# First batch's queries ahead of its keys and values, in an attention and gated feed-forward kernel on one core

## The chip, the cores and the metric

The kernel runs on one core of one Trainium2 chip. The core has five engines with instruction queues of their own: TensorE (PE in the profile, its weight loads PEld), VectorE (DVE), ScalarE (ACT), GpSimd (POOL) and SyncE (SP), which here only issues transfers. Sixteen DMA engines move data between HBM and the core's memory. The metric is device time in microseconds, the median of several runs.

## The reference, cut to what matters

```python
batch, n_heads, seq, head_dim = (8, 8, 576, 64)      # q, k, v, float32

kv  = np.einsum('bhsd,bhse->bhde', k, v)             # one 64x64 state per batch and head
out = np.einsum('bhsd,bhde->bhse', q, kv)
rms = np.sqrt(np.mean(out * out, axis=-1, keepdims=True) + 1e-06)
attn = out / rms * g_norm

x   = attn.transpose(0, 2, 1, 3).reshape(4608, 512)
rms = np.sqrt(np.mean(x * x, axis=-1, keepdims=True) + 1e-06)
xn  = x / rms * rms_g
g   = xn @ w_gate                                    # 512 x 1536
silu = g * (1.0 / (1.0 + np.exp(-g)))
y   = (silu * (xn @ w_val)) @ w_out                  # 1536 x 512
```

There is no softmax: keys and values of a head collapse into a 64x64 state, and each query row is multiplied by it. Two root-mean-square norms follow, one over a head and one over a token, and then a gated feed-forward layer.

## The kernel before, in words

The work goes through nine blocks of 512 tokens: the first 512 tokens of each of the eight batches, and a ninth block of the eight batches' last 64 tokens. For a block n the class `Ffn` computes twelve strips of gate and value products (`up`, L490, matmuls on L496), the gated product (L501 on ScalarE, L502 on VectorE), and four row blocks of down products (`down_products`, L543, matmuls on L548). While one block is in its feed-forward stage, the attention of the next is woven into it. Matrix products take bfloat16 operands, so every loaded float32 tile is cast once, on an engine that each call names.

The order of instructions on each engine is the order of the calls in the program (`tc.manual_schedule()`); nothing is reordered. Semaphores are put in by the framework: a reader waits for the writer of its tile, a tile that takes a pool buffer waits for the last user of that buffer, and a transfer on the hardware queues of SP or ACT waits for the eighth such transfer before it. Which buffer of a pool a tile gets is settled at build time.

The change lies in the start, before the first block's feed-forward stage. There the first batch is handled in pieces:

- Keys and values come in four pairs of heads, j = 0 to 3, 288 KB each (`load_kv`, L118). The first two pairs' keys go on SP's queue and their values on ScalarE's; the later two pairs go on SP's queue alone. `cast_kv` (L122) casts one pair.
- `state0(j, dummies)` (L681) takes a bank of `att_pool`, which has two, puts filler matmuls into it (`warm`, L646, on zeros), and multiplies the pair's keys and values in 18 matmuls of 64x64 (`kv_pair`, L251, matmuls on L256). With dummies = 0 it puts one narrow filler. `put_state0` (L687) copies the state out on VectorE.
- The first 256 queries of the batch come in two transfers of 256 KB (`load_q0(0, ...)`, L609), are cast on VectorE and ScalarE (`cast_q0`), turned by eight matmuls into an `att_pool` bank behind some fillers (`turn_q0`, L665), and put in place by one copy on VectorE and one on ScalarE (`put_q0`, L675). The second 256 queries go the same way later (`load_q0(1, ...)`).
- `columns(A, j, bank)` (L690) multiplies state j by the turned queries; `squares` and `square` square them on ScalarE; `A.sums()` adds the squares up with matmuls; `A.factors()` (L451) makes the norm factors; `scale_both` and `x_turn` then make the first feed-forward input. `Z` is the same for the second 256 queries.
- `gam` holds the two norm weights, turned by one small matmul (L742); from it come `gcol`, `rowscale` (L744) and `gsq`. `rowscale` multiplies every gate and value weight when it is rounded to bfloat16 (`round_w`, L186, on GpSimd L193, ScalarE L191 or VectorE L193).
- The weights follow on SP's queue in pieces of 512 KB and 1 MB (`load_w`, L169): first the strips 0 to 3 of gate (L180) and value (L184), then strips 4 to 7, then the rest, and after them the keys, values and queries of the next batches and the down weights (`load_wo`, L197).

Loaded float32 tiles live in a pool of seven `stage` buffers. The keys and values of the third batch are loaded by `load_pair(2)`, into buffers that earlier loads have left; VectorE and GpSimd cast them at 54 to 60 us.

Of the kernel before, what the change touches and what calls it, by code (L numbers as in the profile page):

```python
# [20 lines left out]
def kernel(  # L21
# [12 lines left out]
    nc = tc.nc  # L34
# [41 lines left out]
    PE, DVE, SC, GP = nc.tensor, nc.vector, nc.scalar, nc.gpsimd  # L76
# [26 lines left out]
    def cast(engine, dst, src):  # L103
        if engine is SC:
            engine.copy(out=dst, in_=src)  # L105
        else:
            engine.tensor_copy(out=dst, in_=src)  # L107
# [10 lines left out]
    def load_kv(b, name, queue, js=slice(0, NS)):  # L118
        view = srcs[name][b].rearrange("h s d -> (h s d)").rearrange("(j p x) -> p j x", j=NS, p=128)
        queue.dma_start(out=raws[b, name][:, js, :], in_=view[:, js, :])  # L120

    def cast_kv(b, name, j, engine, lo=0, hi=C):  # L122

        cast(
            engine, bufs[b][name][:, j, lo:hi].rearrange("p c d -> p (c d)"), raws[b, name][:, j, lo * D : hi * D]
        )
# [124 lines left out]
    def kv_pair(ps, j):  # L251

        for c in range(C):
            for u in range(2):
                rows = slice(u * D, u * D + D)
                PE.matmul(  # L256
                    ps[rows, rows], lhsT=kbs[0][rows, j, c, :], rhs=vbs[0][rows, j, c, :],
                    start=(c == 0), stop=(c == C - 1),
                )
# [349 lines left out]
    def load_q0(f, queue):  # L609

        src = q[0, :, 256 * f : 256 * f + 256, :].rearrange("(g h) (p t) d -> h p g (t d)", h=2, t=8)
        for h in range(2):
            queue.dma_start(out=q0[:, f, h, :], in_=src[h])

    for j in (0, 1):
        load_kv(0, "k", nc.sync, slice(j, j + 1))
        load_kv(0, "v", nc.scalar, slice(j, j + 1))
# [3 lines left out]
        out=gam[NS : NS + 1, :].rearrange("o (i d) -> o i d", i=2),  # L621
        in_=g_norm.rearrange("(o d) -> o d", o=1).unsqueeze(1).to_broadcast([1, 2, D]),
    )
    load_q0(0, nc.sync)
    for j in (2, 3):
        load_kv(0, "k", nc.sync, slice(j, j + 1))
        load_kv(0, "v", nc.sync, slice(j, j + 1))
# [18 lines left out]
    def warm(ps, count, w=512):  # L646
        for _ in range(count):
            PE.matmul(ps[:, 0:w], lhsT=warm_sb[:, 0:128], rhs=warm_sb[:, 0:w], start=True, stop=True, skip_group_check=True)  # L648
# [8 lines left out]
    A = Cols(0, 0, 256, qt0, sqt0, "A")  # L657
# [4 lines left out]
    def cast_q0(f, hs, engine):  # L662
        cast(engine, qb0[:, f, :, hs, :], q0[:, f, hs, :].rearrange("p h (t d) -> p t h d", t=8))

    def turn_q0(f, dummies):  # L665
        bank = att_pool.tile([128, 512], FP32, name="att_ps")
        warm(bank, dummies)
        ps = bank.bitcast(BF16).rearrange("p (t x) -> p t x", t=8)
        for t in range(8):
            PE.matmul(  # L670
                ps[:, t, :], lhsT=qb0[:, f, t], rhs=identity, is_transpose=True, start=(t == 0), stop=(t == 7),
            )
        return ps.rearrange("p t (x g) -> p g t x", g=NS)

    def put_q0(f, ps, i, engine):  # L675

        js = slice(2 * i, 2 * i + 2)
        dst = qt0[:, js, 256 * f : 256 * f + 256].rearrange("p j (t x) -> p j t x", t=8)
        cast(engine, dst, ps[:, js])

    def state0(j, dummies):  # L681
        ps = att_pool.tile([128, 512], FP32, name="att_ps")
        warm(ps, max(dummies, 1), 512 if dummies else 128)
        kv_pair(ps[:, 0:128], j)
        return ps

    def put_state0(j, ps):  # L687
        DVE.tensor_copy(out=kv_all[:, 0, j, :], in_=ps[:, 0:128])

    def columns(cols, j, bank):  # L690
        cols.turned(j, bank[:, 256 * (j % 2) : 256 * (j % 2) + 256])
# [6 lines left out]
    def squares(cols, i, bank):  # L698
        SC.activation(
            out=cols.sq[:, 2 * i : 2 * i + 2, :], in_=bank.rearrange("p (j t) -> p j t", j=2), func=ACT.Square  # L700
        )
# [16 lines left out]
    warm_ps = att_pool.tile([128, 512], FP32, name="att_ps")  # L718
    warm(warm_ps, 9)

    for j in (0, 1):
        cast_kv(0, "k", j, DVE)
        cast_kv(0, "v", j, SC)
    kv0 = state0(0, 0)
    kv1 = state0(1, 3)
    put_state0(0, kv0)
    cast_q0(0, hs0, DVE)
    cast_q0(0, hs1, SC)
    put_state0(1, kv1)
    banksA = [gps_pool.tile([128, MAIN], FP32, name="g_ps"), vps_pool.tile([128, MAIN], FP32, name="v_ps")]  # L730
    qps = turn_q0(0, 2)
    cast_kv(0, "k", 2, DVE)
    cast_kv(0, "v", 2, SC)
    put_q0(0, qps, 0, DVE)
    put_q0(0, qps, 1, SC)
    kv2 = state0(2, 3)
    cast_kv(0, "k", 3, DVE)
    put_state0(2, kv2)
    cast_kv(0, "v", 3, DVE, 0, 5)
    cast_kv(0, "v", 3, SC, 5, C)  # L740
    gam_ps = ops_pool.tile([128, 512], FP32, name="o_ps")
    PE.matmul(gam_ps[:, 0:5], lhsT=gam[0:5, :], rhs=ident32[0:5, 0:5], is_transpose=True, start=True, stop=True)  # L742
    DVE.tensor_copy(out=gcol, in_=gam_ps[:, NS : NS + 1])
    DVE.tensor_scalar(out=rowscale, in0=gam_ps[:, 0:NS], scalar1=gcol[:, 0:1], scalar2=None, op0=OP.mult)  # L744
    columns(A, 0, banksA[0])
    columns(A, 1, banksA[0])
    squares(A, 0, banksA[0])
    columns(A, 2, banksA[1])
    square(A, 2, banksA[1])
    kv3 = state0(3, 1)  # L750
# [17 lines left out]
    qps = turn_q0(1, 2)  # L768
# [336 lines left out]
```

## Time and profile before

| what | value |
|---|---|
| median of 5 runs | 319.05 us (318.86 to 319.52) |
| profiled execution, its own time | 319.15 us |
| its span, first to last instruction | 317.0 us |
| TensorE matmuls busy | 307.8 us, 97% of the span |
| VectorE, ScalarE, GpSimd busy | 179.8, 175.9, 22.7 us |
| moved by DMA | 54.95 MB, mean 173 GB/s |
| mean granted TensorE clock | 0.998 |

The span runs from the first to the last instruction; some 2 us of the run lie around it. A busy TensorE is pipelined work with modelled ends, so 97% says that the engine is hardly ever without work, not that it runs at its peak. In the lists of instructions each row gives a start, a length, the engine, the line of the program, the operation with its output and inputs, and in brackets the idle time of that engine just before it with what ended it. An engine name with a q (SPq) is the engine's queue issuing a transfer; a row named DMA in the chain is the time in which a transfer was under way.

### The profile page before, as it was taken

Reading aid. Unit: us, or ns where it says so; the run is one execution under the profiler, and the core shown is the slowest. Engines: PE = TensorE matmul, PEld = TensorE weight load, DVE = VectorE, ACT = ScalarE, POOL = GpSimd, SP = SyncE. Lnnn points to the kernel's source line nnn. Section 1 sums busy time; section 2 is a strip of 40 time slices with the busy share of each in tenths; the row PEclk is TensorE's granted clock in tenths of the full one; section 3 lists DMA queues with packets and bytes.
Section 4 is the critical chain, followed back from the end, with each engine's and each line's share of the span. In section 5 each row is a group of like instructions: output and inputs, shape, how many; then the busy total and the mean of one; then the engine's idle time right before and its main releaser. Section 6 shows DMA issues by size and latency. Waiting matters only on the chain.

```text
span 317.0 us, 6005 instructions
## 1 busy us (share of the span) xinstructions
PE 307.8 (97%) x2339; PEld 150.5 (47%) x2371; DVE 179.8 (57%) x373; ACT 175.9 (55%) x330; POOL 22.7 (7%) x48
## 2 busy tenths in 40 slices
PE   7899999999999999999999999999999999999995
PEld 3575446444454444444454445444444444444443
DVE  3666768679628922893179416950795079504310
ACT  3677367485878466837683768442744274233321
POOL 2264351100000000000000000000000000000000
PEclk9999999999999999999999999999999999999999
DMA  7999998699669347904790469136003710330014
GB/s 266 379 387 388 375 374 321 162 338 341 158 178 329 128 93 223 373 15 83 205 380 31 71 196 216 52 66 183 18 0 66 153 48 3 63 137 3 0 33 99
DMA packets 60316, 54.95 MB, mean 173 GB/s; under 512 B 36348, under 2 KB 44800, under 8 KB 60288
## 3 DMA queue, kind: packets, MB, share of 16 engines
q1 hardware_dynamic: 59776, 53.85, 54.5%
q10 hardware_dynamic: 448, 0.72, 0.7%
q8 instruction: 18, 0.29, 0.4%
q14 instruction: 10, 0.08, 0.1%
q0 software_dynamic: 64, 0.00, 0.0%
HBM read 37.75 MB, written 9.44 MB: 149 GB/s over the span
## 4 chain that ended last, share of the span: by engine, by line
PE 90%; DMA 5%; another core or an unknown queue 1%; SPq 1%; issue 1%; POOL 1%; DVE 0%; ACT 0%
PE v_ps L496 29%; PE g_ps L496 28%; PE o_ps L548 26%; DMA st<-in_moe_w_val_dram 3%; DMA st<-in_k_dram 2%; PE v_ps L548 1%; PE g_ps L548 1%; PE att_ps L288 1%; DMA out_dram<-o_sb 1%; PE g_ps L288 1%; PE att_ps L328 1%; PE o_ps L513 1%; POOL wv_sb L193 1%; PE o_ps L328 0%
## 5 line engine op out<-in xcount | busy, mean ns | idle before, releaser
L502 DVE TENSOR_TENSOR h_sb<-silu,v_ps 128x512 bf16<-128x512 bf16 x104 | 71.1, 684 | 98.1 <-ACT silu L501 64.8
L496 PE MATMUL v_ps<-xnt,wv_sb 128*128 128x512 bf16 x414 | 106.5, 379 | 0.4
L496 PE MATMUL g_ps<-xnt,wg_sb 128*128 128x512 bf16 x398 | 104.6, 379 | 0.6
L501 ACT ACTIVATE silu<-g_ps 128x512 bf16<-128x512 f32 x104 | 62.1, 597 | 73.4 <-PE g_ps L496 58.2
L548 PE MATMUL o_ps<-wo_sb,h_sb 128*128 128x512 bf16 x386 | 87.1, 379 | 0.5
L496 PEld LDWEIGHTS <-wv_sb 128*128 128x128 bf16 x416 | 40.7, 98 | 49.1
L548 PEld LDWEIGHTS <-h_sb 128*128 128x128 bf16 x420 | 40.5, 98 | 47.4 <-issue 0.4
L496 PEld LDWEIGHTS <-wg_sb 128*128 128x128 bf16 x416 | 40.0, 98 | 47.3
L105 ACT COPY o_sb<-o_ps 128x512 f32<-128x512 f32 (+1 forms) x34 | 19.6, 581 | 41.8 <-PE o_ps L548 39.0
L375 DVE TENSOR_TENSOR xna<-outa,s1y 128x512 bf16<-128x512 bf16 x28 | 17.9, 683 | 0.0
L105 ACT CAST qb<-st 128x512 bf16<-128x512 f32 (+1 forms) x30 | 16.2, 602 | 2.5 <-DMA st<-in_q_dram 2.3
L358 DVE TENSOR_REDUCE ssq<-sq 128x16 f32<-128x1024 bf16 x14 | 17.1, 1220 | 0.5
L358 DVE TENSOR_REDUCE ssq<-sqt 128x16 f32<-128x1024 bf16 x14 | 17.1, 1220 | 0.5
L105 ACT CAST vb<-st 128x576 bf16<-128x576 f32 (+1 forms) x22 | 13.6, 660 | 3.7 <-DMA st<-in_v_dram 3.7
L105 ACT CAST kb<-st 128x576 bf16<-128x576 f32 x20 | 12.4, 673 | 0.0
L343 ACT ACTIVATE sq<-att_ps 128x512 bf16<-128x512 f32 x14 | 7.6, 594 | 4.3 <-PE att_ps L328 3.6
L357 DVE TENSOR_TENSOR sq<-sq,gsq 128x512 bf16<-128x512 bf16 x14 | 5.9, 422 | 4.9 <-ACT sq L343 4.9
L648 PE MATMUL att_ps<-kv_all 128*128 128x512 bf16 (+1 forms) x21 | 7.5, 485 | 1.2 <-DVE sel L636 1.2
L107 DVE CAST kb<-st 128x576 bf16<-128x576 f32 x12 | 6.0, 516 | 3.9 <-DMA st<-in_k_dram 3.9
L107 POOL CAST wo_sb<-st 128x512 bf16<-128x512 f32 x12 | 7.3, 635 | 7.3 <-DMA st<-in_moe_w_out_dram 7.3
L343 ACT ACTIVATE sqt<-o_ps 128x512 bf16<-128x512 f32 x14 | 7.6, 603 | 0.0
L349 ACT CAST outa<-att_ps 128x512 bf16<-128x512 f32 x14 | 7.5, 592 | 0.0
(157 smaller groups left out, 186.4 us busy)
## 6 DMA issues: line engine op xcount, KB each, us to landing
st<-in_k_dram SPq DMA_DIRECT2D x7, 1152.0 KB, 9.9
st<-in_v_dram SPq DMA_DIRECT2D x7, 1152.0 KB, 11.8
out_dram<-o_sb SPq DMA_DIRECT2D x14, 512.0 KB, 2.9
st<-in_q_dram SPq DMA_DIRECT2D x6, 1024.0 KB, 7.2
st<-in_moe_w_out_dram SPq DMA_DIRECT2D x6, 512.0 KB, 10.4
st<-in_moe_w_gate_dram SPq DMA_DIRECT2D x4, 512.0 KB, 9.1
st<-in_moe_w_val_dram SPq DMA_DIRECT2D x4, 512.0 KB, 12.1
out_dram<-o_sb SPq DMA_DIRECT2D x14, 128.0 KB, 4.5
```

The lines of the kernel that those rows point to most:

```text
L105: engine.copy(out=dst, in_=src)
L107: engine.tensor_copy(out=dst, in_=src)
L288: PE.matmul(self.kv_ps[x][to, a, :], lhsT=kb[rows, 2 * a + x, c, :], rhs=vb[rows, 2 * a + x, c, :], start=(a == 0 and c == 0), stop=(a == ...
L343: SC.activation(out=self.in_place(self.sq[i][:, 0], g), in_=bank, func=ACT.Square)
L349: SC.copy(out=self.in_place(rows, g), in_=bank)
L358: DVE.reduce_sum(out=self.ssq[:, c], in_=sq, axis=AX.X)
L375: DVE.tensor_tensor(out=self.xna[c], in0=self.outa[c], in1=self.alpha[:, c, :].to_broadcast([128, H, D]), op=OP.mult)
L496: PE.matmul(ps, lhsT=wt[:, s, j * 128 : (j + 1) * 128], rhs=x[:, s, :], start=(s == 0), stop=(s == NS - 1),)
L501: SC.activation(out=silu, in_=g_ps, func=ACT.Silu)
L502: DVE.tensor_tensor(out=self.h[:, j, :], in0=silu, in1=v_ps, op=OP.mult)
L548: PE.matmul(self.o_ps[c], lhsT=self.h[:, j, c * 128 : (c + 1) * 128], rhs=wo_sb[:, j, :], start=(j == 0), stop=(j == NF - 1),)
L648: PE.matmul(ps[:, 0:w], lhsT=warm_sb[:, 0:128], rhs=warm_sb[:, 0:w], start=True, stop=True, skip_group_check=True)
```

## The change

Two things are done, both in the start.

In the queue of transfers, the two transfers of the first 256 queries move from behind the first two pairs of keys to the very front of SP's queue.

On the engines, the queries are cast, turned and put in place before and between the casts of the first two pairs. The states of pairs 0 and 1 follow behind the turn; the state of pair 2 comes before columns 0 and 1 as before, and the small turn of the norm weights moves behind these columns. The counts of fillers are set anew (one with the turn, then four, two and none instead of none, three, two and three).

```diff
+    load_q0(0, nc.sync)
     for j in (0, 1):
         load_kv(0, "k", nc.sync, slice(j, j + 1))
         load_kv(0, "v", nc.scalar, slice(j, j + 1))
...
-    load_q0(0, nc.sync)
     for j in (2, 3):
         load_kv(0, "k", nc.sync, slice(j, j + 1))
         load_kv(0, "v", nc.sync, slice(j, j + 1))
...
     warm(warm_ps, 9)
 
-    for j in (0, 1):
-        cast_kv(0, "k", j, DVE)
-        cast_kv(0, "v", j, SC)
-    kv0 = state0(0, 0)
-    kv1 = state0(1, 3)
-    put_state0(0, kv0)
     cast_q0(0, hs0, DVE)
     cast_q0(0, hs1, SC)
+    qps = turn_q0(0, 1)
+    cast_kv(0, "k", 0, DVE)
+    cast_kv(0, "v", 0, SC)
+    put_q0(0, qps, 0, DVE)
+    put_q0(0, qps, 1, SC)
+    cast_kv(0, "k", 1, DVE)
+    cast_kv(0, "v", 1, SC)
+    kv0 = state0(0, 4)
+    put_state0(0, kv0)
+    cast_kv(0, "k", 2, DVE)
+    cast_kv(0, "v", 2, SC)
+    kv1 = state0(1, 2)
     put_state0(1, kv1)
     banksA = [gps_pool.tile([128, MAIN], FP32, name="g_ps"), vps_pool.tile([128, MAIN], FP32, name="v_ps")]
-    qps = turn_q0(0, 2)
-    cast_kv(0, "k", 2, DVE)
-    cast_kv(0, "v", 2, SC)
-    put_q0(0, qps, 0, DVE)
-    put_q0(0, qps, 1, SC)
-    kv2 = state0(2, 3)
+    kv2 = state0(2, 0)
     cast_kv(0, "k", 3, DVE)
     put_state0(2, kv2)
     cast_kv(0, "v", 3, DVE, 0, 5)
     cast_kv(0, "v", 3, SC, 5, C)
+    columns(A, 0, banksA[0])
+    columns(A, 1, banksA[0])
+    squares(A, 0, banksA[0])
     gam_ps = ops_pool.tile([128, 512], FP32, name="o_ps")
     PE.matmul(gam_ps[:, 0:5], lhsT=gam[0:5, :], rhs=ident32[0:5, 0:5], is_transpose=True, start=True, stop=True)
     DVE.tensor_copy(out=gcol, in_=gam_ps[:, NS : NS + 1])
     DVE.tensor_scalar(out=rowscale, in0=gam_ps[:, 0:NS], scalar1=gcol[:, 0:1], scalar2=None, op0=OP.mult)
-    columns(A, 0, banksA[0])
-    columns(A, 1, banksA[0])
-    squares(A, 0, banksA[0])
     columns(A, 2, banksA[1])
```

In the program as built, the new order also changes which of the seven stage buffers some later loads take: the keys of `load_pair(2)` take the buffer that the first down weights (`load_wo(0)`) had, and its values take the buffer that the second batch's keys had; before, they took the buffers of the second batch's keys and of its values.

## The prediction

> **What bounds the kernel now.** I read the page's slices first, then the chain that ended last for its first 24 us, then the engines' timelines over the same stretch.
>
> ```profile
> span 317.0 us, 6005 instructions
> ...
> PE   7899999999999999999999999999999999999995
> ...
> DMA  7999998699669347904790469136003710330014
> GB/s 266 379 387 388 375 374 321 162 338 341 158 178 329 128 93 223 373 15 83 205 380 31 71 196 216 52 66 183 18 0 66 153 48 3 63 137 3 0 33 99
> ```
>
> Each slice is 7.9 us. TensorE is full from the third slice to the last; the DMA engines are full from the second to the sixth. The change touches only the first 12 us, so the end moves only if the moment moves at which TensorE becomes full. The chain says what sets that moment (start, length, piece):
>
> ```profile
> 2.36 0.68 SPq L613
> 3.04 0.04 issue
> 3.08 5.67 DMA st<-in_k_dram
> 8.75 0.02 issue
> 8.77 9.59 DMA st<-in_moe_w_val_dram
> 18.35 0.08 issue
> 18.44 1.85 POOL wv_sb L193 x4
> 20.29 0.05 issue
> 20.33 0.50 PE v_ps L522 x3
> ```
>
> It is a stream of transfers: the third pair of keys (issued at 3.08), then the first half of the value weights (issued the moment those keys landed, arriving at 18.35), then GpSimd's rounding of four pieces, then the gate products. No state, query or column of the first batch is on it. From 3.5 us on, the windowed view has the DMA engines at 341 to 415 GB/s in every stretch. So the start is bound by bytes: whatever leaves the order of arrival of the weights alone leaves 18.44 alone.
>
> Beside it runs the chain that the change rearranges (start, length, engine, line, what; in brackets the idle time before):
>
> ```profile
> 8.04 0.62 ACT L105 CAST qb<-st 128x512 bf16<-128x512 f32 x1 [1.25 <-DMA st<-in_q_dram]
> 9.54 0.67 ACT L105 CAST vb<-st 128x576 bf16<-128x576 f32 x1 [0.88 <-DMA st<-in_v_dram]
> 11.02 0.41 ACT L105 CAST vb<-st 128x256 bf16<-128x256 f32 x1 [0.33 <-DMA st<-in_v_dram]
> ...
> 9.37 0.69 DVE L107 COPY qt<-att_ps 128x512 bf16<-128x512 bf16 x1
> 10.26 0.46 DVE L107 CAST kb<-st 128x576 bf16<-128x576 f32 x1 [0.20 <-DMA st<-in_k_dram]
> ...
> 8.71 0.62 PE L670 MATMUL att_ps<-identity,qb 128*128 128x128 bf16 x8 [1.07 <-ACT qb L105]
> 10.26 0.47 PE L256 MATMUL att_ps<-vb,kb 64*64 64x64 bf16 x18 [0.28 <-ACT vb L105]
> ```
>
> ScalarE and VectorE wait for a transfer before nearly every cast. The last pair's values land at 11.02, and the fourth state, last column, sums and factors follow from that landing.
>
> [...] keys on SP's queue and values on ScalarE's land as a pair, at 4.54 and 4.71, then 5.82 and 6.13. [...] ten filler products take 4.12 us from 1.18 (0.41 each), three at 5.84 take 0.82; a 1.07 us gap before 8.71 brought no relapse. [...]
>
> **The change, part by part.** The sum is made against the profiled execution: 319.15 us, of which the span is 317.0 and 2.15 lie around it. The median is 319.05.
>
> *Issue.* SP issued k0, k1 (0.87 for both), q0's two halves (1.40), then k2 at 3.08. Now the 1.40 go before the 0.87; the sum and k2's issue at 3.08 are unchanged. The first SP issue takes 0.68 instead of 0.40, so SP's first bytes may start up to 0.28 later; ScalarE's queue issues v0 at 0.73 as before and keeps the engines fed. I take 0, bounds 0 and +0.28.
>
> *Waits of the issues.* Each hardware-queue transfer waits for the eighth one before it (v3 was issued at 4.90, after v0's landing). With q0 first, k3 waits for q0's first half, v3 for its second, the second query block for k0 and v0, the gate weights for k1 and v1. From the third pair on the partners are the old ones: value weights still wait for k2 and v2. SP runs perhaps 1 us late in between (gate weights at about 8.5 instead of 7.43), with the value weights queued behind it, whose bytes come only after 1 MB of gate weights. At 8.5 still unlanded are k2 to v3 and the second queries, 4 x 288 + 2 x 256 KB = 1,664 KB, 4.3 us of work at the 387 KB/us seen from 8.04 to 11.02 (1,152 KB). Cost 0; without that backlog it would be up to 1.
>
> *Landings.* Cumulated before: 576 KB at 4.71, 1,152 at 6.13, 1,408 at 7.43, 1,664 at 8.04, 1,952 (k2) at 8.77. Now q0 and v0, v1 come first: 1,088 KB, at about 6.0; k0 makes 1,376, about 7.3; k1 1,664, about 8.0. From k2 on, all as before: v2 9.54, k3 10.26, v3 11.02.
>
> *The new order on the engines*, with durations from the same rows. ScalarE casts the second query half 6.0 to 6.62. TensorE turns it 6.67 to 7.29. ScalarE casts v0 to 7.29, puts its queries (0.58) to 7.91, casts v1 to 8.58, then waits for v2. VectorE: k0 7.3 to 7.76, put (0.69) to 8.45, k1 to 8.91, state 0 (0.28) to 9.19, k2 to 9.65, state 1 to 9.95, then waits for k3 at 10.26. TensorE: four fillers after the turn (0.9), state 0 at about 8.2, two fillers, state 1 at 9.1, state 2 when v2 is cast: 10.26, the old time. So VectorE arrives with 0.3 us to spare, and it is v2, k3 and v3 that end last, as before. The query half may be 0.75 late (0.45 between turn and put, 0.3 before k3) before anything past 10.26 moves.
>
> *State 2 and the norm weights' turn around the columns.* In the old program too the third state's products stood ahead of columns 0 and 1 (10.26 against 10.81). What moves is the small turn (L742, 0.22) behind these columns, so columns 0 and 1 come up to 0.1 earlier and the row scale (VectorE 11.45) up to 0.2 later. The scale's first user is GpSimd at 14.12: hidden by 2.4 us. Squares wait for v3's cast on ScalarE (11.02 + 0.41). One filler fewer in all. 0.
>
> *Cover behind that.* If columns and sums did slip: TensorE finishes the gate products before 18.97 and needs five value products (0.11 each) before the one that waits until 20.33 for GpSimd, so it may be 20.33 - 0.55 - 18.95 = 0.83 us late for nothing.
>
> *A side effect far off.* The seven stage buffers are handed out by the builder's own timing, and in the changed program the third batch's keys (k of load_pair(2)) get the buffer of the first down weights instead of the second batch's keys. Their issue, at 39.52, now waits for GpSimd's casts of those weights, 39.30 + 1.18 = 40.48: +0.96. Behind it on SP stand the values' load and the transposes of 54.20. From issue to landing these keys took 14.2 us, to 53.7, in a queue that moved 349 to 408 GB/s from 36 to 53: the backlog absorbs it. Uncovered, they land at 54.7, just before VectorE's cast at 54.76. 0.
>
> Sum: 0, with -0.1 to +0.3 for what I can't price: 319.05 + 0.05, so 319.1.
>
> **Rivals.**
> A. *The stream packs better: faster.* Between 6.13 and 8.77, where the queries land, 800 KB took 2.64 us; at 387 KB/us it would be 2.07. If queries taken first avoid this, all weights come 0.57 earlier: 318.5. For it: 0.9 DMA share between 7 and 8. Against: a landing is that of the slowest of 16 engines, others work ahead, and bytes per window hardly dip (383, 341 GB/s); the second queries show the same at 12 to 13 wherever they stand.
> B. *TensorE falls back to half clock: slower.* Its fillers end at about 5.5 and the turn starts at 6.67: a gap of 1.2 us, up to 1.8 if the query half lands late, then another of 0.7 before 10.26. The old gaps are 1.07 and 0.28. [...] the 2 to 2.8 us of products between 10.26 and 14.5 double; part lies beside other engines' work. Some 1.8 late against 0.83 of cover: +1.0, 320.1. It decides from 0.83 us of delay on. [...]
> C. *Queries land too late and hold the casts behind them.* Beyond 0.75 + 0.83 = 1.6 us it costs; at 2.2 it is +0.6, 319.7. q0 is issued first, so I doubt it.
> D. *The change does nothing because v0 and v1 still come in beside the queries, and v3 ends last*: this is the forecast itself.
>
> **How the numbers follow.** 0.2% of 319.05 is 0.64 us, about what a measurement of this kernel can tell from no change. Forecast 0.66, all of it within; A 0.12, half of it past the bound; B 0.12, nearly all slower; C and an uncovered wait at 40 us together 0.10, half slower. I add 0.02 to faster and 0.03 to slower for what I don't see, out of the forecast's share. Faster 0.08, same 0.73, slower 0.19. The range takes in A in full (318.5 and a little) and B: 318.3 to 320.2; the forecast's own is 318.9 to 319.4.
>
> **What would show it.** Right: k2 issued at 3.1, landing near 8.8; value weights landing at 18.3 to 18.5; state 3's copy at 12.0; the first product of L496 at an unmoved time. Wrong: GpSimd's rounding start moved by more than 0.3 (the stream), ten products of L648 or L670 after 6 us at 0.41 a piece (B), the cast of k3 starting later than its landing (C), or TensorE idle at 55 to 62 us (the keys' buffer).

## The result, and the profile after

The changed kernel takes 320.35 us (median of 31 runs) against 318.98 us for the kernel before (52 runs): ratio 1.0039, 95% interval 1.0026 to 1.0051. It is slower by 1.2 us or somewhat more, outside the predicted range of 318.3 to 320.2. Single executions of either kernel scatter by 2 to 4 us, so a profile shows one draw and only the ratios decide. The profiled execution took 320.26 us with a span of 318.1, against 319.15 and 317.0 before.

The page of the changed kernel, its slices (tenths busy, and the GB/s that the DMA engines moved, in 40 slices of 8 us):

```profile
span 318.1 us, 6002 instructions
...
PE   5989999999999999999999999999999999999995
...
DMA  7999999599759447913691369226003710230014
GB/s 251 321 389 387 381 375 361 138 358 314 193 142 322 176 84 207 367 43 76 189 381 50 67 190 199 78 59 176 31 0 61 148 57 3 60 138 3 0 34 99
```

TensorE has 5 instead of 7 in the first slice. The second slice of the transfers is still marked 9, but it moved 321 GB/s instead of 379: the mark alone does not show that. The chain that ended last (start, length, piece), up to where TensorE is full:

```profile
2.10 6.10 DMA st<-in_k_dram
...
8.21 0.55 SPq L613
...
9.45 7.19 DMA st<-in_moe_w_gate_dram
...
16.82 1.97 POOL wg_sb L193 x4
...
18.83 0.45 PE g_ps L513 x5
...
23.57 1.91 PE o_ps L513 x16
```

Before, k2 and the value weights carried the start. In this execution it is now the first keys (k0), which land at 8.20; the second block of queries is the eighth transfer after them, so SP issues it only at 8.21, and behind it the gate weights at 9.45 (7.43 before). They land at 16.63, and GpSimd begins to round them at 16.82 (14.12 before), so that it comes to the value weights at 19.66 (18.44 before). The first product of the strip that opens the full stretch (o_ps on L513) starts at 23.57; before it started at 22.23. From there to the end of the span it is 294.5 us after and 294.8 before: **the whole loss of this execution, 1.3 us, is there by 24 us.**

The engines' timelines (start, length, engine, line, what; in brackets the idle time before it):

```profile
7.48 0.62 ACT L105 CAST qb<-st 128x512 bf16<-128x512 f32 x1 [4.57 <-DMA st<-in_q_dram]
...
11.86 0.41 ACT L105 CAST vb<-st 128x256 bf16<-128x256 f32 x1 [0.59 <-DMA st<-in_v_dram]
...
8.22 0.46 DVE L107 CAST kb<-st 128x576 bf16<-128x576 f32 x1 [2.87 <-DMA st<-in_k_dram]
...
13.13 0.29 DVE L688 CAST kv_all<-att_ps 128x128 bf16<-128x128 f32 x1 [0.35 <-PE att_ps L256]
...
8.15 0.62 PE L670 MATMUL att_ps<-identity,qb 128*128 128x128 bf16 x8 [2.53 <-ACT qb L105]
```

The second half of the first queries is cast at 7.48, though issued at 1.48 as the second transfer of SP's queue. TensorE idles 2.53 us ahead of the turn. The copy of state 3 moves from 12.05 to 13.13. The windowed view, first after, then before (window, length, busy time and instructions of PE, PEld, DVE, ACT, POOL; then clock, DMA share, GB/s):

```profile
4.00:7.00 3.00, 1.63 (x4) 0.30 (x2) 0.43 (x1) 0.00 (x0) 0.00 (x0) 1.00 1.00 320
...
10.00:14.00 4.00, 3.74 (x76) 2.23 (x73) 2.65 (x12) 2.64 (x7) 0.61 (x1) 1.00 0.84 277
```

```profile
4.00:7.00 3.00, 2.67 (x35) 1.22 (x34) 1.12 (x3) 1.34 (x2) 0.00 (x0) 1.00 1.07 393
...
10.00:14.00 4.00, 3.54 (x63) 2.35 (x65) 2.49 (x13) 2.97 (x8) 0.61 (x1) 1.00 1.08 371
```

The transfers lose in two ways. From 4 to 7 us the engines are busy (share 1.00) and move 73 GB/s less: 3 x 73 = 0.22 MB, 0.56 us at 393. From 10 to 14 us they lack work (share 0.84), since the gate weights were issued late: 4 x 94 = 0.38 MB, 1.0 us at 371. The records of single packets say what slow and busy means. A packet of 2,048 B takes mostly 84 to 89 ns, one of 2,304 B mostly 93 to 107 ns. Among those that start from 4 to 7 us, 24 took over 150 ns after (up to 1.3 us, 10.0 us of engine time together of the 48 there are), against 5 before (2.7 us). The trace records the landing of a transfer in 16 steps, as many as there are DMA engines, and they are read here as one of each engine. Of the second query half's, 12 had come by 5.74 us and the last at 7.46, and the cast starts at 7.48. Before 4 us every kernel of this document has such packets, 7.3 to 13.0 us of them; what differs is whether they go on behind that.

### The profile page after: what moved, and what is told of

It reads as the page before. It is cut to its first block, busy times and chain, and to the rows that moved or that the text cites. A ratio compares the mean times of both kernels' runs of the same rounds, so it can differ in the third digit from the quotient of the medians.

```text
span 318.1 us, 6002 instructions
## 1 busy us (share of the span) xinstructions
PE 307.7 (97%) x2339; PEld 150.5 (47%) x2370; DVE 179.5 (56%) x373; ACT 175.7 (55%) x330; POOL 22.5 (7%) x48
## 2 busy tenths in 40 slices
DMA packets 60316, 54.95 MB, mean 173 GB/s; under 512 B 36348, under 2 KB 44800, under 8 KB 60288
## 4 chain that ended last, share of the span: by engine, by line
PE 91%; DMA 5%; another core or an unknown queue 1%; SPq 1%; issue 1%; POOL 1%; DVE 0%; ACT 0%; POOLq 0%
PE v_ps L496 28%; PE g_ps L496 28%; PE o_ps L548 26%; DMA st<-in_moe_w_gate_dram 2%; DMA st<-in_k_dram 2%; PE g_ps L513 1%; PE v_ps L548 1%; PE g_ps L548 1%; SPq L613 1%; PE att_ps L288 1%; PE g_ps L288 1%; DMA out_dram<-o_sb 1%; PE att_ps L328 1%; POOL wg_sb L193 1%
## 5 line engine op out<-in xcount | busy, mean ns | idle before, releaser
L349 ACT CAST outa<-o_ps 128x512 bf16<-128x512 f32 x14 | 7.5, 591 | 0.0
```

The lines of the kernel that those rows point to most:

```text
L349: SC.copy(out=self.in_place(rows, g), in_=bank)
```

## The experiments

**The theories.** *Stream*: reading the queries first makes the stream of transfers slow in its first microseconds; k0 and the second query half come late, the transfers that wait for them are issued late, and all weights follow. *Clock*: the gap on TensorE ahead of the turn leaves it at half clock, and the slower products make the loss (rival B). What that means shows in the profile before, where the first fillers start 0.43 us apart and those from 5.84 us on 0.21. *Partners*: what costs is which earlier transfer each issue waits for. *Order*: the new order of the engines costs by itself.

The table holds what the runs showed; ratios are against the kernel before, measured together with it, everything else is from each kernel's one profiled execution. "Half" is the start of ScalarE's cast of the second query half; "4-7" and "10-14" are GB/s in these windows; "long" is the engine time of packets over 150 ns that start from 4 to 7 us; "gate" is the issue of the first gate weights; "full" is the start of the first o_ps product on L513.

| kernel | ratio (interval) | half | 4-7 | long, us | gate | 10-14 | full |
|---|---|---|---|---|---|---|---|
| before | 1 | 8.04 | 393 | 2.7 | 7.43 | 371 | 22.23 |
| after | 1.0039 (1.0026-1.0051) | 7.48 | 320 | 10.0 | 9.45 | 277 | 23.57 |
| e0, after again | 1.0050 (1.0032-1.0067) | 6.81 | 332 | 10.7 | 8.73 | 337 | 23.06 |
| j3, after again | 1.0066 (1.0038-1.0094) | 6.99 | 333 | 8.5 | 8.92 | 326 | 23.07 |
| e1, new transfers, old order | 1.0078 (1.0053-1.0103) | 6.48 | 304 | 12.5 | 8.62 | 362 | 23.85 |
| e2, old transfers, new order | 1.0106 (1.0061-1.0150) | 9.23 | 380 | 3.4 | 8.55 | 364 | 26.25 |
| e3, other partners | 1.0037 (1.0021-1.0053) | 7.71 | 313 | 11.7 | 8.94 | 321 | 23.95 |
| f1, gap filled | 1.0052 (1.0031-1.0072) | 7.61 | 346 | 7.3 | 9.94 | 245 | 24.03 |
| f2, fewer fillers | 1.0058 (1.0038-1.0079) | 6.23 | 342 | 7.5 | 8.84 | 320 | 23.06 |
| f3, halves on two queues | 1.0013 (1.0002-1.0025) | 5.04 | 397 | 0.0 | 7.64 | 364 | 22.45 |
| h1, f3 with fillers | 1.0013 (0.9994-1.0033) | 5.63 | 393 | 0.0 | 8.33 | 367 | 22.72 |
| g1, both halves contiguous | 1.0001 (0.9986-1.0016) | 5.75 | 395 | 1.5 | 8.01 | 346 | 21.25 |
| k1, second half contiguous | 1.0030 (1.0014-1.0046) | 5.96 | 344 | 7.8 | 8.91 | 309 | 22.26 |
| k2, first half contiguous | 1.0023 (1.0012-1.0033) | 5.96 | 338 | 7.7 | 8.48 | 357 | 21.45 |
| f4, before, gap filled | 1.0018 (1.0006-1.0030) | 8.30 | 359 | 5.3 | 7.66 | 378 | 21.80 |
| g3, before, few fillers | 1.0014 (0.9997-1.0031) | 8.62 | 374 | 2.8 | 7.97 | 367 | 23.05 |
| g2, before, two queues | 0.9999 (0.9981-1.0018) | 7.83 | 367 | 4.8 | 7.63 | 373 | 21.75 |
| j4, before, spread keys | 1.0019 (1.0006-1.0032) | 8.02 | 359 | 6.9 | 7.97 | 373 | 21.75 |

### The two parts apart: e0, e1, e2, e3

e0 is the changed kernel, unedited.

> The changed kernel again, for its spread and a second trace. If the long packets at the start of the stream are what the new order brings, the second query half lands again a microsecond or more after the first (4.9 and 7.5 in the trace at hand), with a few of the sixteen DMA engines late, and the gate weights land after 15.5; if they were chance of one execution, it lands near 6.0 and the span is near 317.3. Time: 0.3 to 0.5% above the kernel before.

e1 has `load_q0(0, nc.sync)` ahead of the keys, and the casts, turns and states in the order of before.

> The transfers in the new order, the engines in the old one. Transfer theories (issue partners, or a slower stream): the loss is here, about +1.0 to +1.3 us as in the whole change. Engine-order theory (the casts held behind the queries on ScalarE and VectorE are what costs): this one is at the time of the kernel before, within 0.4 us.

e2 leaves the transfers where they were and has the new order of the engines:

```diff
-    load_q0(0, nc.sync)
     for j in (0, 1):
...
+    load_q0(0, nc.sync)
     for j in (2, 3):
```

> The engines in the new order, the transfers in the old one, so that the casts of the first two pairs wait on VectorE and ScalarE until the queries land at 7.4 and 8.0. By my durations VectorE then reaches the last cast 1.2 us late, 0.83 of it covered: +0.4 us. Transfer theories: no more than that, with value weights landing at 18.4 as before. Engine-order theory: +1.0 us or more, from the late columns.

e3 puts ScalarE's two loads of values ahead of the queries in the program. Order and place on each queue stay, but each later transfer counts back to another eighth one:

```diff
+    for j in (0, 1):
+        load_kv(0, "v", nc.scalar, slice(j, j + 1))
     load_q0(0, nc.sync)
     for j in (0, 1):
         load_kv(0, "k", nc.sync, slice(j, j + 1))
-        load_kv(0, "v", nc.scalar, slice(j, j + 1))
```

> The changed kernel with the same queues in the same order, but ScalarE's first values issued ahead of the queries in the program, which changes only the partners of the waits for the eighth transfer before: the last values' issue waits for the first query half instead of the second, the second queries' for the second half, the gate weights' for the first keys. Issue-partner theory: the fast DMA engines are no longer starved between 10 and 14 us (share back from 0.84 to 1.0) and at least 0.6 us comes back. Slow-stream theory (the late engines are late by themselves): the share rises but the landings of the late engines and the time stay, within 0.3 us of the changed kernel.

Transfers alone cost 1.0078, the order alone 1.0106, both together 1.004 to 1.007. The order alone is bad for a plain reason: it waits for queries that come late, with TensorE idle 4.53 us until the turn at 9.91. Its products are at half clock from there on (clock 0.50 from 10 to 14 us), and it lost 3.4 us where the durations had promised 0.4. By itself the order costs nothing: g1, further down, has it, and no loss. It is the transfers that bring the slow stream: 304 to 333 GB/s from 4 to 7 us wherever the queries come first (e0, j3, e1, e3), 380 where they don't (e2). Other partners (e3) change nothing that can be told: as a theory of its own, *partners* falls. That says nothing against late issues as the way in which a slow stream is passed on; in e3 the gate weights still went out at 8.94.

In e0's execution TensorE did go to half clock, as in those of e1, e2 and e3: the granted clock was 0.68, 0.87, 0.73 and 0.72 from 7 to 10 us, and 0.82, 0.67, 0.50 and 0.79 from 10 to 14. In j3's the record says 1.00 in both windows, but the turn took 1.03 us instead of 0.62, and the four fillers behind it 1.91 instead of 1.03. The timeline of e0:

```profile
7.48 0.62 PE L670 MATMUL att_ps<-identity,qb 128*128 128x128 bf16 x8 [2.28 <-ACT qb L105]
7.94 1.79 PE L648 MATMUL att_ps<-kv_all 128*128 128x512 bf16 x4
9.66 0.69 PE L256 MATMUL att_ps<-vb,kb 64*64 64x64 bf16 x18
```

Four fillers take 1.79 us instead of 1.03, a state 0.69 instead of 0.47. So what rival B feared does occur, here behind a gap of 2.28 us and a turn that still took 0.62. In the profiled execution of the result, a gap of 2.53 brought none of it.

These products are also on the chain that ended last in e0, and the weights are not. Its chain, and GpSimd's first rounding of value weights:

```profile
1.47 5.31 DMA st<-in_q_dram
...
6.81 0.63 ACT qb L105
...
7.48 0.62 PE att_ps L670 x8
8.10 1.63 PE att_ps L648 x4
9.73 0.62 PE att_ps L256 x11
10.35 0.97 PE att_ps L648 x2
...
23.06 1.91 PE o_ps L513 x16
```

```profile
17.38 2.83 POOL L193 TENSOR_SCALAR wv_sb<-st,rowscale 128x256 bf16<-128x256 f32 x6
```

GpSimd begins with the value weights 1.1 us earlier than in the profile before (18.44), and TensorE is full 0.8 later all the same: the late second query half holds the turn, and the slower products behind it do the rest. The chain of j3, the same kernel once more, runs the same way (value weights at 18.38, full at 23.07), and so does that of e3; in e1 and f2 it starts from the late first keys. So the slow stream is passed on in two ways, through the weights in the profile of the result and that of f1, and through the late queries or keys and TensorE's half clock in these five.

### Is it the clock? f1, f2, g3, f4

f1 puts seven more fillers into the gap: `turn_q0(0, 1)` becomes `turn_q0(0, 8)`.

> The changed kernel with eight fillers instead of one ahead of the queries' turn, so that TensorE is busy until about 7.1 instead of 5.5 while it waits for the second query half. Clock theory (the gap drops TensorE to half clock in most executions, and the turn, fillers and states behind it then take twice as long): no filler of 0.41 us after 7 us, and 0.7 us or more comes back. Landing theory (only the late query half and the casts behind it cost): nothing comes back, within 0.3 us of the changed kernel, or it is slower.

f2 takes the fillers out that stand before the states: `state0(0, 4)` and `state0(1, 2)` become `state0(0, 0)` and `state0(1, 0)`.

> The changed kernel without the four and two full fillers ahead of states 0 and 1 (one narrow one each is left). They are 2.5 us of the chain where TensorE is at half clock and 1.3 where it is not. If they are what makes the late query half costly: about 0.8 to 1.5 us back, to within 0.4 us of the kernel before. If the weights' stream sets the end in most executions: within 0.3 us of the changed kernel.

g3 takes fillers out of the kernel before: 9 fillers become 1, those of `state0(1, 3)` and `state0(2, 3)` go, `turn_q0(0, 2)` becomes `turn_q0(0, 1)`.

> The kernel before with nearly all of TensorE's fillers of the start taken out (warm products 9 to 1, those behind the first keys' chunk 3 to 0, those of the queries' turn 2 to 1, those behind the last early chunk 3 to 0); transfers and engine order stay. The output is the reference's. It prices half clock in the start with undisturbed transfers. If half clock alone carries the changed kernel's loss: states at 0.69 us instead of 0.35 and the first full work of TensorE about 1 us later, 320 us or more. If the early chain's cover of some 0.8 us absorbs it: value weights' rounding still at 18.4, time within 0.2% of before, 318.6 to 319.6.

f4 fills the gap of the kernel before, `turn_q0(0, 7)`.

> The kernel before with seven fillers instead of two ahead of the turn, which closes its gap of 1.07 us before 8.7 (five at 0.21 are 1.07 us of work). If falling to half clock is also what makes a third of its own executions 1.2 us longer (319.6 to 320.6 against 318.2 to 319.2): these vanish, the median stays within 0.3 us of 318.6. If they come from the transfers: they stay, and the time is the same or up to 0.3 us longer.

f1 is no faster, 1.0052. Its execution has no half clock (the turn 0.62, the four fillers 1.03, behind a gap that is still 1.65 us), but the result's profile had none either. And fillers have a price of their own: f4, the kernel before with five more, is slower, 1.0018 (1.0006 to 1.0030), which neither theory had foretold. If f1's seven cost as much, an estimate of 0.6 us, about 1.1 us of f1's loss remains without them. f2 is no faster either, but it doesn't take half clock away: the granted clock was 0.62 from 7 to 10 us and 0.50 from 10 to 14. g3 prices half clock with an undisturbed stream (374 GB/s from 4 to 7 us): its turn takes 1.03 us instead of 0.62, as its timeline shows, and its states 0.69 instead of 0.47 up to 13 us, yet it loses 0.45 us, with an interval from nothing to 1.0.

```profile
9.29 1.03 PE L670 MATMUL att_ps<-identity,qb 128*128 128x128 bf16 x8 [1.24 <-ACT qb L105]
```

So half clock is a part of the loss in those executions where it comes; how large a part over all executions, these runs don't show, and f1 only makes it likely that it isn't the whole. What f1 kept is the slow stream, with 346 GB/s, gate weights issued at 9.94 and 245 GB/s from 10 to 14; its chain runs through value weights that land at 20.15 (18.35 before). That profile is the slowest of f1's nine executions.

### Is it the stream? f3, h1, g2

f3 sends the second query half through ScalarE's queue, ahead of its values:

```diff
-            queue.dma_start(out=q0[:, f, h, :], in_=src[h])
+            (nc.scalar if f == 0 and h == 1 else queue).dma_start(out=q0[:, f, h, :], in_=src[h])
```

> The changed kernel with the second query half on ScalarE's queue, ahead of the values, instead of second on SP's. Landing theory: both halves land by about 4.5, TensorE turns them at about 5.2 with no gap, and the loss is gone: within 0.3 us of the kernel before. If the first reads of keys and values later in the stream are what costs, the values and keys land late instead and the loss stays at 0.8 us or more.

h1 is f3 with `state0(1, 7)`, to fill a gap of 1.13 us that f3 has ahead of its second state.

> The changed kernel with the queries' second half on ScalarE's queue ahead of the values, and seven fillers behind the second chunk's state instead of the few it has, to bridge the 1.13 us gap ahead of the second state that was seen with the split alone. If what remained of the loss with the split alone (ratio 1.0013) is half clock behind that gap: no product of double time in the first 15 us, ratio 1.000 or less. If it is the later weights and keys (issues moved behind the queries): ratio stays at 1.001 to 1.002.

g2 is the same edit as f3's in the kernel before, where it puts that half behind ScalarE's values.

> The kernel before with the queries' second half issued on ScalarE's queue behind its values instead of on SyncE's behind the first half; engine order stays. If two halves on one queue hold each other up whenever they are issued: the second half lands at least 0.5 us earlier than the 8.02 us of before, and the time is the same or up to 0.2% less, since the start of before is bound by the bytes up to the value weights (18.35 us). If the late second half is a matter of the stream's first microseconds alone: landings as before within 0.3 us, 318.9 us.

f3 brings back two thirds and more. Its windows:

```profile
4.00:7.00 3.00, 2.60 (x16) 1.05 (x14) 1.51 (x3) 1.21 (x3) 0.00 (x0) 1.00 1.03 397
10.00:14.00 4.00, 3.83 (x60) 2.50 (x60) 2.43 (x11) 2.28 (x6) 0.61 (x1) 0.71 1.08 364
```

The stream is as fast as before, no packet is long from 4 to 15 us, the second half is cast at 5.04, the gate weights go out at 7.64, and the DMA engines do not run dry from 10 to 14 (share 1.08). Half clock is there all the same (clock 0.71 from 10 to 14), without taking much. h1 has none of it behind its turn (four fillers 1.03, granted clock 1.00) and the same ratio, with an interval too wide, and five fillers more, to say whether the remainder is the clock. g2 is the kernel before to within the measurement.

### Is it where the queries are read? g1, k1, k2, j4, j1, j2

Beside its place, one thing sets the queries' transfers apart from the keys'. Keys are read in consecutive rows, partition after partition. A query transfer (`"(g h) (p t) d -> h p g (t d)"`) gives each four neighbouring partitions 2 KB from four heads that lie 288 KB apart.

g1 is the changed kernel, reading consecutive rows for the first 256 queries. These are then the wrong queries, so it serves for the time alone:

```diff
+        if f == 0:
+            src = q[0].rearrange("h s d -> (h s d)")[0:131072].rearrange("(h p x) -> h p x", h=2, p=128)
         for h in range(2):
             queue.dma_start(out=q0[:, f, h, :], in_=src[h])
```

> The changed kernel with one difference: the two transfers of the first queries read contiguous rows (2 KB to a partition, as those of the keys do) instead of every row's four heads; so the first 256 queries are read from the wrong places and the output is not the reference's; bytes, packets, queue and place on it are as in the changed kernel. If the pattern of the queries' reads makes some of the 16 DMA engines late: second half lands about 6.0 us, few packets over 150 ns between 3 and 7 us, and at least 0.7 us back (about 319.6 or less). If it is the place on the queue, whatever is read: second half lands 6.8 to 7.7 us, time as the changed kernel's, about 320.4.

The loss is gone: 1.0001, with an interval that overlaps with none of the three of the changed kernel, which was measured three times, though never beside g1. One more thing differs with the addresses: SP issues g1's queries in 0.88 us instead of 1.33, so the first keys go out at 1.64 instead of 2.10. That doesn't explain the stream, for by 4 us the changed kernel had moved no fewer bytes (282 and 338 GB/s from 2 to 3 and 3 to 4 us, against 203 and 400 in g1). Windows and chain of g1:

```profile
4.00:7.00 3.00, 2.19 (x13) 0.86 (x12) 0.76 (x2) 1.19 (x2) 0.00 (x0) 1.00 1.04 395
...
10.00:14.00 4.00, 3.80 (x67) 2.47 (x61) 2.35 (x13) 2.58 (x7) 0.61 (x1) 1.00 1.05 346
```

```profile
9.20 8.15 DMA st<-in_moe_w_val_dram
...
17.44 1.86 POOL wv_sb L193 x4
...
21.25 1.91 PE o_ps L513 x16
```

This is nearly the course that the prediction described: second half at 5.75 (forecast 6.0), the value weights back as the bound. They even land at 17.35, and TensorE is full 1.0 us earlier than in the profile before. Yet the span is 317.6, not 316. A later wait gave the 1.0 back, 70 us on (timeline of TensorE, then the rows of the turned queries by g1 and by before, transfers from issue to landing):

```profile
94.52 0.29 PE L328 MATMUL o_ps<-kv_all,qt 64*128 64x64 bf16 x8 [1.25 <-DMA qt<-qb]
```

```profile
DMA to landing us min/median/max: 2.5/2.6/4.4
```

```profile
DMA to landing us min/median/max: 2.4/2.5/2.5
```

One of four transposing transfers took 4.4 us instead of 2.5. The same wait stands in the profiles of f1 (0.76), f4 (0.67) and j4 (0.83), and in none of before, after, f3 or g2. So it comes and goes between executions; whether an early start makes it likelier wasn't tried.

k1 and k2 have consecutive rows for one half each: `rows[h] if (f, h) == (0, 1) else src[h]` in k1, `(0, 0)` in k2.

> The changed kernel with contiguous rows for the second half of the first queries alone (its queries are then read from the wrong places; the first half's stay right). If it is the second half's own spread reads that make a few DMA engines late: it lands about 6.0 us, ratio about 1.000 as with both halves contiguous. If the first half's reads do it, or the place on the queue: it lands at 6.8 to 7.7 us, ratio 1.004 or more.

> The changed kernel with contiguous rows for the first half of the first queries alone (wrong places for that half, the second stays right). If the second half's own spread reads make it late: it lands at 6.8 to 7.7 us, ratio 1.003 or more. If the first half's reads do: about 6.0 us and 1.000.

Neither theory of these two was right. In both profiles the second half lands on time (cast at 5.96), but the stream is still slow from 4 to 7 us, with 344 and 338 GB/s and 7.8 and 7.7 us of long packets, and the ratios lie between g1's and the changed kernel's, with intervals that overlap with some of these. So the spread reads of *either* half slow the stream, and a late second half is not the whole of the loss: part of it stays where that half is on time. In which way it is passed on there, the two profiles don't show, for TensorE is full in them no later than before (22.26 and 21.45).

j4 puts the pattern elsewhere, on the first two pairs of keys in the kernel before:

```diff
+        if b == 0 and name == "k" and js.stop - js.start == 1 and js.start < 2:
+            apart = k[0].rearrange("h s d -> (h s d)").rearrange("(g j p x) -> j p g x", g=4, j=4, p=32)
+            queue.dma_start(out=raws[b, name][:, js.start, :], in_=apart[js.start])
+            return
```

> The kernel before, with the first two pairs of keys read in the queries' spread pattern (four places 288 KB apart instead of consecutive rows), so they take other rows of the keys and the output is not the reference's; bytes, packets, queue and place stay. If the pattern makes engines late whatever is read: the keys of the first two pairs land 0.5 us or more after the 4.5 and 5.7 us of before, long packets go on past 3 us, ratio above 1.001. If it is something of the queries alone: landings as before, ratio 1.000.

The first keys landed as before (cast at 4.41), the second, behind them on SP's queue, 0.9 late (cast at 6.75 instead of 5.82); 6.9 us of long packets, 359 GB/s, ratio 1.0019. This points to the pattern and not to the queries as such, but weakly: other kernels that read the keys' rows first had 359 to 380 GB/s as well (f4, g2, g3, e2), so that figure tells nothing, and f4 has the same ratio for another reason. The late landing is what speaks for it.

j1 and j2 were meant to keep the results and still read 64 KB in consecutive rows: `"(g h) (p t) d -> h g p (t d)"` for the load and `"p t (g x) -> p g t x"` behind the turn, in the changed kernel (j1) and in the one before (j2). j3 was measured beside them.

> The changed kernel, with the first batch's queries laid out so that 32 neighbouring partitions take 64 KB of consecutive rows of one head, instead of every partition's neighbours taking rows of four heads 288 KB apart; the put behind the turn picks its columns to match. Same queries, bytes, packets of 2,048 B, queue and place; the output is the reference's. If the spread reads made the DMA engines late: second half lands about 6.0 us, few packets over 150 ns from 3 to 7 us, no half clock, ratio 1.000 or less. If they did not: as the changed kernel beside it, 1.004.

> The kernel before with the same layout of the first batch's queries. If spread reads cost wherever they stand: the queries' second half lands up to 0.5 us before the 8.02 us of before, the value weights at about 17.4 instead of 18.35, ratio 0.997 to 0.999. If they cost only at the stream's start: 1.000. The output is the reference's.

> The changed kernel once more, beside the regrouped one on the same chip. By both theories as before: ratio 1.003 to 1.005, second query half landing at 6.8 to 7.7 us. If it comes out at 1.000, the contiguous kernels' times say nothing on the reads.

Both lost 11 us: j1 1.0361 (1.0333 to 1.0390), j2 1.0369 (1.0339 to 1.0399). They say nothing on the reads, since they changed something else. The transfers line of the page of j1, and then that of before, tells what:

```profile
DMA packets 60268, 54.95 MB, mean 167 GB/s; under 512 B 36300, under 2 KB 44752, under 8 KB 60240
```

```profile
DMA packets 60316, 54.95 MB, mean 173 GB/s; under 512 B 36348, under 2 KB 44800, under 8 KB 60288
```

48 small packets are missing, all of them under 512 B, at the same 54.95 MB. What they may be, the trace of before shows: beside the landings, in 16 steps each, stand packets of 4 B, 46 that end from 14 to 18 us beside 46 steps. If all that is missing belongs to the four edited transfers, each has 12 fewer; that each of them went over 16 - 12 = 4 engines instead of 16 is an estimate from that. The engines did lack work: their share from 10 to 14 us was 0.55 at 162 GB/s, against 1.08 at 371 before. The chain of j1 shows the price, the second block of queries:

```profile
13.55 10.96 DMA st<-in_q_dram
```

From issue to landing 256 KB of queries took 11.0 us; the median of such a transfer in the kernel before is 5.8.

## Why the prediction was wrong

The prediction said 319.1 us with 0.73 on no change; it is 1.2 us or more slower, on the side that had 0.19.

*What bounds the kernel* held in one half: the end moved with the moment at which TensorE becomes full (1.3 us there, 1.1 in the span). That bytes alone set this moment did not hold. In e0 and j3 it moved by 0.8 though the value weights were not late. And in the profile before, 15 of the 16 engines had the first half of the value weights in by 16.54 us, and only the last one ended at 18.35; after, 15 had the first gate weights by 15.06, the last at 16.63. What holds one engine back by 1.6 to 1.8 us was not tried.

*Issue* held, k2 went out at 3.09 (forecast 3.08).

***Landings* is the step that failed.** It added up bytes and put them on the times at which before had moved as many, so that the queries and two pairs of values would be there "at about 6.0", k0 at 7.3 and everything from k2 on as before. That takes the stream's speed as given, whatever is read first. With the spread reads first it is 304 to 346 GB/s from 4 to 7 us instead of 393, and the second half came at 6.2 to 7.7, k0 at up to 8.7. g1, with other addresses, gave 395 GB/s and the forecast's time. I looked at bytes and queues and not at the pattern of the reads, though the profile before held a hint: it was the queries' transfers, from 6.13 to 8.77, that took 2.64 us for what the usual rate does in 2.07. Rival A read that very hint as a gain to be had.

*Waits of the issues*, priced at 0 with the gate weights at about 8.5, failed as a consequence: with both parts of the change they went out at 8.7 to 9.9, and the engines moved 245 to 337 GB/s from 10 to 14 us instead of 371. The backlog that was to cover this ran out in the result's profile (DMA share 0.84) and hardly in e0's (0.99). The step itself had said that without backlog it costs up to 1.

*The new order on the engines* had 0.75 us to spare for the query half and 0.83 of cover behind. By that count 1.46 late (7.46 against 6.0) was just covered. In the profiled execution it was, and the gate weights set the end. In e0 and j3 only 0.8 and 1.0 late (6.81 and 6.99) was too much, because the products behind ran at half clock (four fillers 1.79 and 1.91 us instead of 1.03), which this step's count left out.

Of the rivals, *B* happened (half clock behind gaps of 2.28 and 2.03 us, where 1.2 to 1.8 had been feared), and it lay on the chain that ended last in e0 and j3. That a gap of 1.2 to 1.8 us would do was the author's estimate: behind 1.49, 1.58 and 1.65 us (k2, k1, f1) the turn took 0.62 us and four fillers 1.03, behind 1.86 (f2) the turn took 0.62 and the states after it 0.69. Its 320.1 comes near the result, partly by luck: it took the queries to be up to 0.6 us late and knew nothing of the slow stream behind, and in the result's own profile there is no half clock. *C* named the late queries, doubted them because they are issued first, and gave 319.7; it had the symptom right and not the stream behind it. The far-off wait for a stage buffer cost nothing, as forecast: TensorE does not idle at 55 to 62 us.

**What stays open.** Why spread reads make long packets at the head of the stream, and why the same reads make none after 4 us when the halves go through two queues (f3), no run shows. How the loss divides between late weights and half clock isn't measured either. No version that keeps the results beat both kernels: g2 equals the one before, and f3, the best with the queries first, is slower by 0.13%.

## What to carry to other kernels

Before a transfer is moved to the head of a stream, look at what it reads as well as at how much: a load of 2 KB pieces from places far apart can make the whole stream slower while the DMA engines show busy (320 GB/s at a share of 1.00 from 4 to 7 us, against 395 at 1.04 with consecutive rows), and what waits for an early transfer is then issued late (the gate weights at 9.45 us instead of 8.01). Read the GB/s beside the DMA share in short windows, for the share alone hides it. When two bounds lie close together (TensorE was full at 23.57 by way of the weights, and at 23.06 by way of the queries), work on one of them can bring nothing back; the experiment that counts is the one that changes the common cause. And one profile shows one way of losing: the same kernel profiled again showed another.

## What was not expected of the hardware

- Single packets of 2 KB took up to 1.3 us instead of some 84 ns in the first microseconds of a stream, 24 of 430 from 4 to 7 us, some more while the second queries land (9 to 13 us), and none from 19 to 24. With other addresses (g1) the 10.0 us of such time from 4 to 7 us became 1.5. Of the 24, 18 were packets of keys and values (2,304 B).
- A new layout of four transfers of 256 KB, out of 55 MB, cost 11 us in 319 (j1, j2). That they went over 4 engines instead of 16 is an estimate from the 48 packets that j1 has fewer.
- Half clock did not go by the length of the gap alone. In e0 the turn behind a gap of 2.28 us took 0.62 us and the four fillers after it 1.79; in j3, behind 2.03, they took 1.03 and 1.91; in the result's profile, behind 2.53, 0.62 and 1.03. In f3 a state at 11.57 us took 0.63 us, after 0.47 for the one at 10.26, and the longest gap since the turn was 1.13.
